# The second quarter of the pole tables: loaded back from DRAM in round 3 or in round 7

## The chip, the core and the metric

The kernel runs on one core of a Trainium2 chip. A core has a matrix engine (TensorE, in the profile PE, with its weight loads as PEld), a vector engine (VectorE, DVE), an engine for activation functions (ScalarE, ACT), a general engine (GpSimd, POOL) and one that mainly issues DMAs (SyncE, SP). Each engine runs its own instructions in order and waits on semaphores for the others. DMAs are issued from an engine's instruction stream and carried out by 16 DMA engines that all queues share; in this kernel SP's loads go through one queue (q1 in the profile) and POOL's through another (q0).

The metric is the time of one execution in microseconds of device time, as the median of several runs; lower is better.

## The reference

The program normalizes its input with a modulated layer norm, runs it through a long convolution whose kernel comes from a state-space model (S4), adds the result, and passes that through a gated MLP with a spatial gate. What matters here is how the convolution kernel `K` comes out of the poles, for D = 576 channels, N = 128 poles a channel and L = 2048 steps:

```python
dt = jnp.exp(log_dt)[:, None]
A = A_re + 1j * A_im
Bc = B_re + 1j * B_im
Cc = C_re + 1j * C_im
logdA = dt * A
dB = dt * Bc
l = (lambda x, dt: x.astype(dt))(jnp.arange(L), A_re.dtype)
P = jnp.exp(logdA[:, :, None] * l[None, None, :])
K = jnp.einsum("dn,dnl,dn->dl", Cc, P, dB).real
...
y = (lambda x, s, axes=(-2,-1): jnp.fft.irfft2(x, s=s, axes=axes))(Yf, (1, L2), axes=(-2, -1))[:, :, 0, :L]
y = (lambda x, *d: x.transpose(*d))(y, 0, 2, 1) + u * Dskip[None, None, :]
```

`Yf` is the product of the spectra of `K` and of the normalized input `u`.

## The kernel before

The kernel has two large stages. The function `ssm` computes the convolution and takes somewhat over 400 us; the class `Mlp` then does the gated MLP in the rest of the time. The change lies in `ssm`.

**The pole tables.** For each pole `poles` works out the real exponent, the phase for one step, the phase for 64 steps, and the weight's logarithm and phase. To keep precision it splits each number into three bf16 parts, and it stores these into two DRAM buffers, `pa_d` for phases and `pb_d` for exponents. `poles` is called twice: for the first quarter of the channels (`p0`), and for the other three quarters together (`p1`), which is a generator that the main loop advances a little in each of its first rounds; its last stores are recorded in round 2. All these stores are DMAs on POOL.

`poles_load(c, Q)` (line 296) reads one quarter back, in the layout that TensorE needs as weights: three tiles of 112 partitions by 9 groups of 128 poles, `lb` (exponents), `lc` and `la` (phases), each with two DMAs of 48 partitions, and one memset of the unused middle rows of `lb`. The queue `Q` is POOL's. The pool of these tiles has two buffers a name, so two quarters can stand in memory.

**The main loop** (line 703) runs over rounds, called `tick`, of which 36 start a new group of 16 channels each, and a quarter has nine groups. A group `g` passes through these steps:

- `e_unit` (L450 to L454): TensorE multiplies `lb` with a selection table into PSUM, ACT takes the exponential into `et`. It is done for three groups at a time, in every third round.
- `t_unit` (L467 to L484): TensorE forms phases out of `lc` and `la` (L467; for the first ten groups with a rounding trick, L471, and a DVE copy, L479; later with L482 on ACT and L483 on DVE), and L484 clears the sign for the cosine.
- `s_unit`, one round later (L489, L490): sine and cosine on ACT, in place in `ft`.
- `p_unit`, two rounds later (L500 to L503): products of `et` and `ft` on DVE.
- `kg_unit`, `d_unit`, `k1_unit` (L513 to L537): small products on TensorE, copies on ACT and an addition on DVE that give the group's convolution kernel and its first transform, `k1`.

Exponentials and sines are in different tables of ACT, so that ACT loads a table (ACT_TABLE_LOAD) when it changes between them.

In the first eight rounds the loop also normalizes the input. `ln_load` fetches `ln_x` and `mod_load` fetches rows of modulation weights, `wm`, both on SP; `ln_pair` (L433, L435) transforms two blocks and stores them into `u1_d` with two DMAs on POOL (L436, `u_d<-st1o` in the profile); `mod_unit` in rounds 3 to 5 works out a modulation row and stores it with one DMA on POOL (L372, `mod_d<-gar`). From round 9 on the loop loads constants `cst` and the transformed input `u` on SP, and from round 10 on come the steps of the convolution itself: `u_unit` (L580, L581; two DMAs on POOL, L582 and L583, exchange the halves of `uu`), `z_unit` (L592, L593), `v_unit` (L600 to L603). `st4` (round 16, `st<-in_c_st` in the profile) and the first MLP weights, `wst`, are loaded on SP in the same stretch of time.

**What sets the order.** A scheduler places the recorded instructions on each engine, except those issued through `mlp.tied`, which keep the order of the program among each other. The DMAs of `poles` and `poles_load` are tied, the stores of `ln_pair` and `mod_unit` aren't. A DMA on POOL also waits until the DMA eight places before it has landed, since eight completion counters are used in turn.

The second quarter is first needed by group 9, that is by `e_unit(9)` to `e_unit(11)` and `t_unit(9)` of round 9. Before the change it is loaded at the end of round 7.

Of the kernel before, what the change touches and what calls it, by code (L numbers as in the profile page):

```python
# [164 lines left out]
def ssm(tc, I, x1_d, consts_s, dram, mod_d, mlp):  # L165
# [5 lines left out]
    with ExitStack() as ctx:  # L171
# [124 lines left out]
        def poles_load(c, Q):  # L296
            for n, d_, k in (("lb", pb_d, 0), ("lc", pa_d, 0), ("la", pa_d, 3)):
                t_ = tb.tile([112, 9, 128], BF, name=n)
                if n == "lb":
                    Q.memset(t_[32:64], 0.0)  # L300
                for h in range(2):
                    Q.dma_start(t_[64 * h:64 * h + 48], d_[c, h, k:k + 6].rearrange("q (c g n) -> (q c) g n", c=8, g=9))
                lt[n, c] = t_
# [22 lines left out]
        def mod_load(k):  # L326

            if k < 2:
                t = kp.tile([128, 32, 128], F32, name="k1").rearrange("p a b -> p (a b)")
                wmt[k] = [t[:96, 6 * HC * hh:6 * HC * hh + 6 * HC].rearrange("p (k n) -> p k n", k=6) for hh in range(2)]  # L330
            else:
                wmt[k] = [ep.tile([96, 6, HC], F32, name="wm") for hh in range(2)]
            for hh in range(2):
                S.dma_start(wmt[k][hh], I["w_mod"][:, k, hh])
# [7 lines left out]
        def mod_unit(k):  # L342
            wm = wmt.pop(k)
            mpart = ep.tile([128, D], F32, name="mpart", bufs=1)
            pm = ps2()
            for hh in range(2):
                for kt in range(6):
                    j = kt % 4
                    T.matmul(pm[32 * j:32 * j + 32, hh, :HC], ec[:, kt:kt + 1].to_broadcast([96, 32]),
                             wm[hh][:, kt], start=kt < 4, stop=kt >= 2, skip_group_check=True)  # L350
            A.activation(v3(mpart), pm[:, :, :HC], AF.Copy)
            pm = ps2()
            for hh in range(2):
                T.matmul(pm[:, hh, :HC], ones, mpart[:, HC * hh:HC * hh + HC], start=True, stop=True)
            src = pm[:, :, :HC]
            if k == 2:
                A.activation(v3(gar), src, AF.Copy)
            elif k == 1:
                V.scalar_tensor_tensor(v3(cga), src, 1.0, v3(gar), op0=ALU.add, op1=ALU.mult)
            elif k == 0:  # L360
                V.tensor_tensor(v3(sga), src, v3(gar), op=ALU.mult)
                for i in range(2):
                    A.activation(gsp, sga, AF.Copy)
                    V.scalar_tensor_tensor(sga, gsp, msk[:, i:i + 1], sga, op0=ALU.mult, op1=ALU.add)
                A.activation(gsp, sga, AF.Copy)
            else:
                mrow = ep.tile([128, D], F32, name="gar", bufs=1)
                if k == 4:
                    A.activation(v3(mrow), src, AF.Identity, bias=one)
                else:  # L370
                    A.activation(v3(mrow), src, AF.Copy)
                G.dma_start(mod_d[k - 3:k - 2], mrow[0:1])  # L372
# [5 lines left out]
        def ln_load(i):  # L378
            x4s[i] = ep.tile([128, 4, D], F32, name="ln_x")
            S.dma_start(x4s[i], I["x"][:, 4 * i:4 * i + 4])  # L380
# [42 lines left out]
        def ln_pair(b):  # L423
            pair = [ln_rows(b), ln_rows(b + 1)]
            for h in range(2):
                c = slice(HC * h, HC * h + HC)
                o = ep.tile([128, 4, HC], F32, name="st1o")
                pms = [ps2(), ps2()]
                for t, (n, rt, cs) in enumerate(pair):
                    for x, y, st in ((cs, gsp, True), (rt, n, False)):  # L430
                        for g in range(4):
                            rows = slice(32 * g, 32 * g + 32)
                            T.matmul(pms[g // 2][64 * t:64 * t + 64, g % 2, :HC], x[rows], y[rows, c], start=st, stop=not st, skip_group_check=True)  # L433
                for k, pm in enumerate(pms):
                    A.activation(o[:, 2 * k:2 * k + 2], pm[:, :, :HC], AF.Copy)  # L435
                G.dma_start(u1_d[:, b:b + 2, :, :, c].rearrange("g b r k d -> (b r k) g d"), o)  # L436
# [7 lines left out]
        def e_unit(g):  # L444
            c, gi = divmod(g, 9)
            lb = lt["lb", c]
            e = et[g] = tb.tile([128, 1536], F32, name="et", bufs=5)
            pa = ps2()
            for h, (l, r) in enumerate(zip(halves(lb, gi), rows(256, 512))):
                T.matmul(pa[:, h], l, r, start=True, stop=True)  # L450
            A.activation(e[:, :1024].rearrange("p (h n) -> p h n", h=2), pa, AF.Exp)
            pb = ps1()
            T.matmul(pb, lb[:, gi], sel[:, 1024:1536], start=True, stop=True)
            A.activation(e[:, 1024:], pb, AF.Exp)  # L454
# [113 lines left out]
        def cst_load(kg):  # L568
            cst[kg] = cs.tile([128, 8, 128], F32, name="cst%d" % kg)
            S.dma_start(cst[kg], I["c_st"][:, 8 * kg:8 * kg + 8])  # L570
# [132 lines left out]
        for tick in range(NG + 4):  # L703
            if tick == 9:
                early.close()
                cs = ctx.enter_context(tc.tile_pool(name="cs", reuse_waits="tile", bufs=1, side="right"))
                sb = ctx.enter_context(tc.tile_pool(name="sb", reuse_waits="tile", bufs=2, side="right"))
                wpre = ctx.enter_context(tc.tile_pool(name="wpre", reuse_waits="tile", bufs=2, side="right"))
            if 9 <= tick < 13:
                cst_load(tick - 9)  # L710
            if tick == 16:
                st4 = cs.tile([128, 16, 2, 64], F32, name="st4")
                S.dma_start(st4, I["c_st4"])
            if tick in (20, 24):
                mlp.start_load(tick // 4 - 5, wpre)
            todo = plan.get(tick, [])

            def go(fn):
                for f, a in todo:
                    if f is fn:  # L720
                        f(*a)

            def lag(fn, n):
                if 0 <= tick - n < NG:
                    fn(tick - n)

            if tick == 0:
                for g in range(3):
                    e_unit(g)
            go(y_load)  # L730
            go(u_load)
            es = iter(range(tick, tick + 3) if tick % 3 == 0 and 0 < tick < NG else ())

            def e_one():
                for g in es:
                    e_unit(g)
                    break

            if tick < 10:
                go(z_unit)  # L740
                lag(p_unit, 2)
                lag(t_unit, 0)
                lag(s_unit, 1)
                go(v_unit)
                lag(kg_unit, 3)
                go(u_unit)
                lag(k1_unit, 4)
                go(y_unit)
                lag(d_unit, 3)
                if tick == 0:  # L750
                    T = nc.tensor
                for _ in range(3):
                    e_one()
            else:
                go(z_unit)
                lag(p_unit, 2)
                lag(t_unit, 0)
                lag(s_unit, 1)
                lag(kg_unit, 3)
                lag(k1_unit, 4)  # L760
                go(y_unit)
                go(v_unit)
                e_one()
                go(u_unit)
                lag(d_unit, 3)
                e_one()
                e_one()
            if tick < 5:
                next(p1, None)
                next(p1, None)  # L770
            if tick == 0:
                mod_load(3)
            if 3 <= tick < 6:
                mod_unit(tick)
                if tick < 5:
                    mod_load(tick + 1)
            j = tick
            if j < 8:
                if j in (2, 4):
                    ln_stats(j // 2 + 1)  # L780
                ln_pair(2 * j)
                if j < 6:
                    r1_load(j + 2)
                if j in (1, 3):
                    ln_load(j // 2 + 2)
            if tick in (7, 13, 21):
                poles_load(1 + (tick > 7) + (tick > 13), mlp.tied.gpsimd)


        tabs.close()  # L790
# [1429 lines left out]
```

## Time and profile before

| | |
|---|---|
| time, median of 3 runs | 1779.78 us (1778.59 to 1780.67) |
| the profiled execution: its time | 1784.37 us |
| the profiled execution: its span | 1782.6 us |
| mean granted clock of TensorE | 0.967 |
| busy: PE | 1669.4 us (94%) |
| busy: DVE | 1259.5 us (71%) |
| busy: ACT | 832.1 us (47%) |
| busy: POOL | 244.5 us (14%) |

All times inside the profile are microseconds from the start of the span. A line of the timeline gives the start, the busy time, the engine, the line of the kernel, the operation, what it writes and reads, its shapes and how many alike were merged; in brackets stands how long the engine was idle just before, and what it was that ended this. A line of the list of waits says who waited for whom, the sum in microseconds, how many times, and the longest. A line of the list of DMA issues gives the queue, the count, the size of one, and the median time from issue to landing.

### The profile page before, as it was taken

The page shows a single profiled execution, that of the slowest core. Times are in us where ns is not written, and L with a number is a line of the kernel's source. Part 1 is how long each engine was busy: PE and PEld are TensorE (multiplying, and loading weights), DVE is VectorE, ACT ScalarE, POOL GpSimd, SP SyncE. Part 2 cuts the span into 40 slices and gives each one's busy share as a digit, 9 for nine tenths or more (in the row PEclk, how much of TensorE's full clock was granted, in tenths as well). Part 3 has the DMA queues.
Part 4 walks back from the last instruction along what each step waited for, and adds up shares of the span by engine and source line. Part 5 has one row for each costly group of instructions (what it writes and reads, how often), then busy time and mean ns, then how long its engine had stood idle before and what let it go on. Part 6 is the DMA issues. An engine that isn't in the chain of part 4 may idle for free.

```text
span 1782.6 us, 36406 instructions
## 1 busy us (share of the span) xinstructions
PE 1669.4 (94%) x15174; PEld 1247.6 (70%) x15174; DVE 1259.5 (71%) x2259; ACT 832.1 (47%) x1118; POOL 244.5 (14%) x400
## 2 busy tenths in 40 slices
PE   3687899997899999999989999999999999999999
PEld 1243556665455445777878888888888888888887
DVE  6874899966898998688899677688344478344432
ACT  4766998844567656445434444234222223122210
POOL 3322232333122211000000000000111100111100
PEclk9587999998999999999999999999999999999999
DMA  9466646679688779767665886873767573556531
GB/s 259 134 178 184 188 121 181 184 216 294 205 255 259 248 230 266 285 245 251 233 222 165 278 302 244 269 247 124 250 219 231 195 235 98 192 195 217 193 111 40
DMA packets 183381, 376.24 MB, mean 211 GB/s; under 512 B 39360, under 2 KB 103488, under 8 KB 182448
## 3 DMA queue, kind: packets, MB, share of 16 engines
q1 hardware_dynamic: 140416, 175.23, 32.5%
q0 software_dynamic: 36896, 172.01, 29.3%
q10 hardware_dynamic: 5904, 26.67, 3.7%
q8 instruction: 119, 1.95, 0.5%
q14 instruction: 46, 0.38, 0.1%
HBM read 263.11 MB, written 101.31 MB: 204 GB/s over the span
## 4 chain that ended last, share of the span: by engine, by line
PE 65%; DVE 14%; DMA 7%; ACT 5%; issue 5%; POOL 2%; SPq 1%; ACTq 0%; DVEq 0%; POOLq 0%
PE ps L152 53%; PE pz L152 2%; DVE zset L152 2%; PE pk L513 2%; DVE bsz L152 2%; PE pk L530 2%; DMA wsst<-in_w_spT 1%; PE pk L592 1%; DVE gt L152 1%; DMA ln_x<-in_x 1%; DMA zset<-set_d 1%; PE pk L600 1%; DVE wsp L152 1%; DVE n L152 1%; DVE rq L152 1%
## 5 line engine op out<-in xcount | busy, mean ns | idle before, releaser
L152 PEld LDWEIGHTS <-zset 128*128 128x128 f16 x7182 | 702.7, 98 | 92.8 <-DVE zset L152 8.1
L152 PE MATMUL ps<-wsp,zset 128*128 128x256 f16 x6048 | 668.9, 273 | 7.1 <-DVE zset L152 6.5
L152 PE MATMUL pz<-wz,nt 128*128 128x512 f16 (+1 forms) x1120 | 224.1, 360 | 12.9 <-ACT nt L152 5.9
L152 PEld LDWEIGHTS <-nt 128*128 128x128 f16 x1120 | 109.5, 99 | 121.3 <-ACT nt L152 7.5
L152 ACT ACTIVATE z<-gt 128x1024 f16<-128x1024 f32 x56 | 59.0, 1054 | 289.6 <-DVE gt L152 289.6
L152 DVE SCALAR_TENSOR_TENSOR gt<-ps,sc,bsp 128x512 f32<-128x512 f32 x36 | 27.0, 749 | 205.0 <-PE ps L152 203.3
L1928 POOL DMA_DIRECT2D zset<-set_d x96 | 50.8, 530 | 869.7 <-PE ps L152 616.3
L152 PE MATMUL ps<-wout,z 128*128 128x288 f16 x1344 | 170.0, 286 | 0.0
L152 PEld LDWEIGHTS <-z 128*128 128x128 f16 x1344 | 131.5, 98 | 33.0
L152 DVE TENSOR_TENSOR raw<-raw 128x512 f32<-128x512 f32 (+2 forms) x228 | 119.1, 528 | 13.6 <-DMA raw<-z_d 9.3
L152 PE MATMUL ps<-n2o,zset 128*128 128x256 f16 x1134 | 128.2, 273 | 0.0
L152 DVE SCALAR_TENSOR_TENSOR gt<-ps,sc,gt 128x512 f32<-128x512 f32 (+1 forms) x180 | 122.2, 696 | 7.6
L152 DVE TENSOR_TENSOR zset<-raw,zset 128x1792 f16<-128x1792 f32 x48 | 96.9, 2019 | 14.3 <-ACT zset L152 14.3
L152 ACT ACTIVATE zset<-raw 128x1792 f16<-128x1792 f32 x48 | 81.1, 1690 | 54.7 <-PE ps L152 22.2
L152 DVE TENSOR_TENSOR z<-ps,z 128x512 f32<-128x512 f32 (+1 forms) x126 | 71.9, 598 | 36.8 <-ACT z L152 25.0
L152 ACT ACTIVATE wsp<-raw,sc 128x1792 f16<-128x1792 f32 x25 | 44.6, 1784 | 42.7 <-DVE raw L152 35.0
L152 ACT ACTIVATE z<-z,sc 128x1024 f32<-128x1024 f32 x21 | 24.1, 1148 | 75.6 <-DVE z L152 71.9
L152 ACT ACTIVATE z<-pz,sc 128x512 f32<-128x512 f32 (+1 forms) x96 | 51.7, 581 | 13.1 <-PE pz L152 7.1
L152 ACT ACTIVATE z<-z,nm,r 128x1152 f32<-128x1152 f32 x24 | 31.5, 1342 | 52.0 <-DVE nm L152 30.7
L152 PE MATMUL ps<-n2q,wf 128*128 128x512 f16 x252 | 55.7, 379 | 0.0
L501 DVE TENSOR_TENSOR pg<-et,ft 128x1024 f32<-128x1024 f32 x36 | 43.8, 1217 | 12.8 <-ACT ft L489 12.7
L152 DVE BATCH_NORM_STATS2 bsz<-z 128x6 f32<-128x384 f32 x96 | 48.4, 546 | 6.2 <-ACT z L152 5.8
(357 smaller groups left out, 2473.0 us busy)
## 6 DMA issues: line engine op xcount, KB each, us to landing
zset<-set_d POOLq DMA_DIRECT2D x96, 896.0 KB, 4.9
raw<-z_d SPq DMA_DIRECT2D x48, 512.0 KB, 5.6
set_d<-zset ACTq DMA_DIRECT2D x24, 896.0 KB, 5.9
z_d<-z POOLq DMA_DIRECT2D x32, 576.0 KB, 9.6
zset<-wa_d POOLq DMA_DIRECT2D x18, 896.0 KB, 4.9
raw<-in_w_spT SPq DMA_DIRECT2D x25, 512.0 KB, 4.3
set_d<-zset SPq DMA_DIRECT2D x12, 896.0 KB, 5.3
u_d<-st1o POOLq DMA_DIRECT2D x16, 576.0 KB, 4.2
```

The lines of the kernel that those rows point to most:

```text
L152: return self.tc.keep_in_program_order(f(*a, **k))
L501: V.tensor_tensor(pr, pi, c3[:, :, None, :].to_broadcast([128, 16, 2, 32]), op=ALU.mult)
L513: T.matmul(pm[32 * j:32 * j + 32, 64 * i:64 * i + 64], x_[:, c], y_[:, c].rearrange("p s j -> p (s j)"), start=st, stop=not st, skip_group ...
L530: T.matmul(pm[64 * ri:64 * ri + 64, 128 * i:128 * i + 128], kk[:, i], r1[ri], start=True, stop=True, skip_group_check=True)
L592: T.matmul(pm[:, w * j:w * j + w], cst[k // 8][:, k % 8], k1t[c][:, k, :w], start=True, stop=True)
L600: T.matmul(pm, inva, zz[:, 0], start=True, stop=False)
L1928: self.nc.gpsimd.dma_start(o, self.set_d[f, j - 1] if j else self.wa_d[f])
```

## The change

```diff
@@ -783,8 +783,8 @@
                     r1_load(j + 2)
                 if j in (1, 3):
                     ln_load(j // 2 + 2)
-            if tick in (7, 13, 21):
-                poles_load(1 + (tick > 7) + (tick > 13), mlp.tied.gpsimd)
+            if tick in (3, 13, 21):
+                poles_load(1 + tick // 10, mlp.tied.gpsimd)
```

`poles_load(1)` is called at the end of round 3 instead of round 7. The calls of rounds 13 and 21 load quarters 2 and 3 as before (13 // 10 = 1 and 21 // 10 = 2). The function is the same, so one memset and six DMAs of 108 KB each are moved; none is added or removed.

The order of instructions in the built program changes as follows.

- POOL: the memset and the six DMAs stand after the two stores of `ln_pair` in round 3 and ahead of ten DMAs that came before them until now: two of `mod_d` and eight of `u_d`.
- PE: the phases of group 9 (L471, L467 with `lc` and `la`) come right after those of group 8, and the exponents of groups 9 and 10 (L450, L453) follow directly; before, these products were mixed with the small products L513 and L530 of earlier groups, and the phases of group 9 came in pieces.
- DVE: L479 of group 9 comes before the products L500 to L503 of group 8 instead of after them.
- ACT: L489 and L490 of group 8 come before the copy L537; the exponentials of groups 9 to 11 are not interrupted; L516, L537 and L581 come after the sines of group 9 and no longer ahead of L482 of group 10.
- SP: the first 1 MB load of `wst` is ahead of one load of `u` and no longer behind it, and another load of `u` moves between two loads of `wst`.

## The prediction

> **What bounds the kernel now.** I read the page first, then busy time and granted clock by stretch, then the waits around 155 to 215 us, and last the single instructions there.
>
> ```profile
> span 1782.6 us, 36406 instructions
> ```
>
> ```profile
> 160.00:165.00 5.00, 0.58 (x1) 0.10 (x1) 3.12 (x4) 1.75 (x2) 0.96 (x2) 0.50 1.03 285
> 165.00:170.00 5.00, 4.49 (x67) 2.33 (x70) 0.00 (x0) 2.00 (x3) 0.00 (x0) 0.50 1.07 294
> 170.00:180.00 10.00, 9.21 (x138) 5.08 (x130) 4.50 (x6) 8.00 (x10) 1.04 (x2) 0.86 0.53 155
> ...
> 220.00:260.00 40.00, 37.22 (x514) 22.01 (x512) 37.93 (x48) 37.09 (x51) 8.56 (x16) 1.00 0.37 108
> ```
>
> The columns are the stretch, its length, then busy us of PE, PEld, DVE, ACT and POOL, the granted TensorE clock, the DMA share and GB/s. From 220 to 260 three engines are busy for 37 to 38 of 40 us, DVE most: nothing there can be made up, so time lost or won earlier is carried on. From 160 to 170 all stand nearly idle and only the DMA engines are full. The waits (us in total, times, longest) and the instructions name the cause:
>
> ```profile
> PE ps L450 <- DMA lb<-pb_d: 7.6, 2, 7.0
> ```
>
> ```profile
> DVE ft L479 <- PE ps L467: 10.1, 1, 10.1
> ```
>
> ```profile
> ACT et L451 <- PE ps L450: 7.9, 3, 4.4
> ```
>
> ```profile
> 164.34 0.58 PE L450 MATMUL ps<-sel,lb 48*128 48x512 bf16 x1 [7.04 <-DMA lb<-pb_d]
> ```
>
> ```profile
> 173.20 1.23 DVE L479 COPY ft<-ps 128x1024 f32<-128x1024 f32 x1 [10.08 <-PE ps L467]
> ```
>
> ```profile
> 156.30 1.08 POOL L152 MEMSET lb<- 32x1152 bf16 x1
> 157.67 1.31 POOL L152 DMA_DIRECT2D lb<-pb_d  x2 [0.29 <-POOL lb L152]
> ```
>
> ```profile
> 159.96 1.00 POOL L152 DMA_DIRECT2D la<-pa_d  x2
> ```
>
> The second quarter is fetched from 157.7 us and wanted at once. PE waits 7.0 + 0.6 us for it, ACT 7.9 us for PE, and DVE stands 10.1 us before it can copy the tenth group's phases (L479).
>
> **The change part by part.** Moved are one memset and six DMAs, two each for `lb`, `lc` and `la`. The built order puts them on POOL behind the store pair of round 3, ahead of ten stores which they followed before. Here are that place and what lies around it (PE's `wm` products are those of the last modulation row, `mod_unit(5)`), then DMA landings (count, KB each, us from issue to landing):
>
> ```profile
> 89.39 3.74 POOL L152 DMA_DIRECT2D pa_d<-pt  x6 [1.25 <-DVE mv L409]
> ```
>
> ```profile
> 103.00 0.52 POOL L372 DMA_DIRECT2D mod_d<-gar  x1 [9.11 <-ACT gar L371]
> ```
>
> ```profile
> 107.44 0.76 POOL L436 DMA_DIRECT2D u_d<-st1o  x1 [1.44 <-ACT st1o L435]
> ```
>
> ```profile
> 113.91 0.53 POOL L372 DMA_DIRECT2D mod_d<-gar  x1 [5.71 <-ACT gar L369]
> ```
>
> ```profile
> 115.09 1.18 DVE L408 BATCH_NORM_STATS2 bs<-ln_x 128x6 f32<-128x288 f32 x3 [5.30 <-DMA ln_x<-in_x]
> ```
>
> ```profile
> 108.93 1.30 SPq L334 DMA_DIRECT2D wm<-in_w_mod  x2
> ```
>
> ```profile
> 124.48 2.62 PE L349 MATMUL ps<-wm,ec 96*32 96x288 f32 x18
> ```
>
> ```profile
> u_d<-st1o POOLq DMA_DIRECT2D x1, 576.0 KB, 9.7
> ```
>
> ```profile
> wm<-in_w_mod SPq DMA_DIRECT2D x1, 648.0 KB, 11.1
> ```
>
> ```profile
> 110.00:120.00 10.00, 6.63 (x106) 3.49 (x95) 4.91 (x14) 8.80 (x13) 1.72 (x3) 1.00 1.00 330
> ```
>
> Issue: by the rows at 156.30 to 159.96 the block takes 1.08 + 0.29 + 1.31 + 1.00 + 1.00 = 4.7 us of POOL. It starts at 108.2 (107.44 + 0.76) and ends near 112.9, before the `mod_d` store that came at 113.91 after 5.7 idle us. Cost 0; without that cover 4.7 us on a store that nothing reads until the next stage. Can the block itself hang? It reads what `poles` stored, whose last DMA issue ended at 93.1 (89.39 + 3.74), and each DMA takes the completion counter of the one eight places ahead of it; the youngest of these is the `mod_d` store of 103.0. Both are old by 109. A knock-on: the first `u_d` store behind the block takes the counter of the store that lands at 117.1 (107.44 + 9.7), about 1 us after it would go out. Its tile is rewritten only in round 5, near 133 us: cost 0.
>
> DMA traffic: 6 x 108 = 648 KB now come into the stretch 110 to 120, which is full already (share 1.00). The neighbour to fear for is `ln_x`: it lands at 115.1 and DVE stands 5.3 us for it. At that stretch's 330 GB/s 648 KB are 2.0 us, the upper bound; the lower bound is 0. Which end? In the old place the POOL loads came in by order of issue:
>
> ```profile
> lb<-pb_d POOLq DMA_DIRECT2D x2, 108.0 KB, 6.8
> ```
>
> ```profile
> la<-pa_d POOLq DMA_DIRECT2D x2, 108.0 KB, 8.9
> ```
>
> `lb`, out from 157.7, is in at about 165; `la`, out from 160.0, at about 169. So in the new place they stand behind the `u_d` store on POOL's queue, which lands at 117.1, after `ln_x`. I take 0 and keep 2.0. `wm`'s second half goes out at 109.6 (108.93 and half of 1.30), lands at 120.7 and is used at 124.5, so 2.0 us there are hidden.
>
> The Trainium skill, DMA: Bandwidth & Descriptors, section Queues, rings and completion order, says that each DMA engine takes turns between the queues that have work, a packet at a time, and starts what is in one ring in order. By it the POOL queue already holds its turn with the `u_d` store, so `ln_x` loses nothing until 117 (0 in the sum); had that queue been empty, the turns would cost up to the 2.0. The row of `la` behind `lb` agrees with the second half of this.
>
> What is won: in the built order PE makes the tenth group's phases (L471, L467) and the exponents (L450, L453) right behind the ninth group's phases, and ACT does L489, L490, L537, a table load, three pairs L451 and L454, then L482. ACT becomes what sets the pace, since PE's pieces in it are under 2 us each. Its rows, with those of the next steps:
>
> ```profile
> 158.38 1.15 ACT L489 ACTIVATE ft<-ft,consts_s 128x1024 f32<-128x1024 f32 x1 [0.43 <-DVE ft L484]
> ...
> 160.49 1.28 ACT L451 ACT_TABLE_LOAD   x1
> 166.15 1.02 ACT L451 ACTIVATE et<-ps 128x1024 f32<-128x1024 f32 x1 [4.38 <-PE ps L450]
> 167.07 1.08 ACT L454 ACTIVATE et<-pk 128x512 f32<-128x512 f32 x2
> ...
> 175.27 0.60 ACT L581 ACTIVATE uu<-pk 128x512 f32<-128x512 f32 x1 [0.34 <-PE pk L580]
> 175.76 1.11 ACT L482 ACTIVATE ft<-ps,consts_s 128x1024 f32<-128x1024 f32 x1
> ...
> 180.19 1.09 ACT L482 ACTIVATE ft<-ps,consts_s 128x1024 f32<-128x1024 f32 x1
> ```
>
> ```profile
> 184.07 2.07 PE L592 MATMUL pk<-k,cst 128*128 128x128 f32 x8 [4.86 <-ACT k L537]
> ```
>
> ```profile
> 186.93 1.22 DVE L593 TENSOR_TENSOR zz<-pk,uu 128x1024 f32<-128x1024 f32 x1
> ```
>
> ```profile
> 176.16 0.53 POOL L582 DMA_DIRECT2D uu<-uu  x1 [15.20 <-ACT uu L581]
> ```
>
> ```profile
> uu<-uu POOLq DMA_DIRECT2D x2, 128.0 KB, 7.2
> ```
>
> From 158.38: L489 and L490 take 2.11 (160.49 - 158.38), L537 0.49 (as L581 to L482, 175.76 - 175.27), the table load 1.3, three pairs at 0.92 (167.07 - 166.15) plus 0.49, together 4.2. L482 starts at 166.5 instead of 175.76: 9.3 us earlier. The next L482 came 4.43 later (180.19 - 175.76); the new order puts L516, L537 and L581 ahead of it, at most 3 x 0.49, say 1.3. So 166.5 + 4.43 + 1.3 = 172.2 against 180.19: 8.0 earlier. PE's first `z_unit` (L592) came 3.88 after that and comes at 176.1: also 8.0 earlier.
>
> But what is late next? DVE's L593 needs L592, done at 178.1 (176.1 + 2.07), and the swapped halves of `uu`. L581 now goes at 171.7 (172.2 - 0.49); the two swap DMAs follow it by 0.9 and 1.4 (176.16 and half a microsecond more, against 175.27), so the second is out at 173.1. Landing took 7.2 us while `st4` and the `wst` loads were in flight, and these move along with the swap: it lands at 180.3. L593 then runs at 180.3 instead of 186.93: 6.6 us earlier. An unloaded queue would bring the halves before 178.1, and the wait of 2.2 us would be gone.
>
> Sum: DVE is the busiest engine of the stretch that follows, so its 6.6 are carried; 0 for POOL, 0 for `ln_x`. The profiled execution took 1784.37 us, 1.8 more than its span; less 6.6 it would be 1777.8. The runs' median is 4.6 lower than that execution, and I assume the same shift there: **1779.78 - 6.6 = 1773.2 us.** Lower gain: PE's own wait 7.6, less 2.0 for `ln_x`, less 2.2 for the swap, 3.4: 1776.4. Upper gain: all of DVE's 10.1: 1769.7.
>
> On SP one 1 MB `wst` load now precedes a `u` load that is used several rounds later: 0; 1 MB takes 3 us at 330 GB/s, and if the rounds between did not cover them, they would be the price. At 157 to 170 the `u` and `cst` loads lose a competitor of 648 KB; the first `u` was not what ACT waited for (0.34 at L581): 0.
>
> **The rivals.** *Absorbed.* Another operand takes the stall's place, in the conv stage or where that stage hands over to the gated MLP, or the loads still come late. For it: DMA is full from 155 to 170 with `u` and `cst` as well. Against: PE waited for `lb` alone there, and POOL's new place has no late wait. Time 1779.8, unchanged.
>
> *Slower: TensorE's clock.* The clock row shows 0.50 from 160 to 170 and 0.86 from 170 to 180. Should the new pattern of short PE bursts keep it at half speed into the full stretch behind 200 us, PE's 37.22 busy us of 40 (at 1.00) would become 74, a loss of 34 us per 40. The gain is eaten after 6.6 / 34 x 40 = 8 us of half clock there, and it is slower by over 3.6 from 12 us on; 15 us would give 1779.8 + 6 = 1786. For it: the clock does fall after each idle piece. Against: with far more idle time before it, it was at 1.00 from 220 on, and the change takes idle time away.
>
> On that, the Trainium skill (TensorE: Matmul & The Clock Gate, Part 1: The HAM clock gate) says that an idle window of some 3.4 us halves the clock and a like time of steady work restores it. The 0.50 behind the 7.04 us gap agrees; by this rule the half clock cannot last 12 us in a full stretch.
>
> **How the numbers follow.** A measurement of this kernel tells about 0.2%, 3.6 us, from no change. Forecast (gain 3.4 to 10.1): 0.80. A gain beyond 10.1, if the removed idle time also spares cold TensorE work: 0.03. Absorbed: 0.12. Slower: 0.05. So faster 0.83, same 0.12, slower 0.05. The likeliest case's own range, 1769.7 to 1776.4, already holds 0.80; I give 1769.0 to 1776.5.
>
> **What would show it.** Right: the `lb` load is issued on POOL near 109 us; DVE's wait for `ln_x` stays near 5.3 (7.3 would be the upper bound of the contention); no wait of PE for `lb` and none of 10 us before L479; first L592 near 176 us; DVE waits about 2 us for `uu` before its first L593; everything behind 200 us is the old profile shifted by 6 to 8 us. Wrong: a wait of 3 us or more at another place between 110 and 200, a shift at 220 us that is gone at 450, or a clock below 1.00 from 220 to 260.

## The result and the profile after

The changed kernel took 1770.2 us (median of 7 runs, 1765.67 to 1773.18) beside 1778.8 us for the kernel before on the same chip (7 runs, 1775.77 to 1780.67). The ratio is 0.9947, with a 95% interval of 0.9932 to 0.9962: 0.53% or some 9 us faster. The prediction was 1773.2 us in a range of 1769.0 to 1776.5, a gain of 6.6 us.

The profiled execution took 1773.18 us.

```profile
span 1771.4 us, 36409 instructions
```

The first view is the one by stretches, as before the change: length, busy us of PE, PEld, DVE, ACT and POOL, granted clock, DMA share, GB/s.

```profile
160.00:165.00 5.00, 3.51 (x87) 2.12 (x84) 4.99 (x7) 4.49 (x6) 0.00 (x0) 1.00 1.03 302
165.00:170.00 5.00, 4.21 (x80) 2.39 (x83) 1.05 (x3) 4.98 (x8) 0.00 (x0) 1.00 1.05 339
170.00:180.00 10.00, 5.83 (x60) 3.40 (x48) 9.45 (x12) 9.57 (x13) 1.47 (x3) 0.83 0.79 270
...
220.00:260.00 40.00, 37.78 (x518) 22.26 (x516) 36.89 (x46) 37.09 (x49) 12.26 (x22) 1.00 0.40 114
```

The hole from 160 to 170 is filled: in its first half DVE and ACT are busy for 4.99 and 4.49 of 5 us (3.12 and 1.75 before), in its second ACT for 4.98 (2.00). DMA is as full as it was, and TensorE's clock is at 1.00 there instead of 0.50. Next, the waits from 105 to 205 us (who for whom, sum, times, longest):

```profile
DVE bs L408 <- DMA ln_x<-in_x: 4.9, 1, 4.9
...
DVE ft L479 <- PE ps L467: 3.6, 3, 1.6
...
POOL u_d L436 <- DMA u_d<-st1o: 2.7, 1, 2.7
PE ps L450 <- ACT et L451: 2.6, 2, 1.3
```

No wait of PE for `lb` is left, and DVE's longest wait for the phases is 1.6 us where it was 10.1. POOL's new place, on the timeline:

```profile
104.77 0.52 POOL L372 DMA_DIRECT2D mod_d<-gar  x1 [9.62 <-ACT gar L371]
...
109.96 1.08 POOL L152 MEMSET lb<- 32x1152 bf16 x1
111.33 1.06 POOL L152 DMA_DIRECT2D lb<-pb_d  x2 [0.29 <-POOL lb L152]
112.39 0.99 POOL L152 DMA_DIRECT2D lc<-pa_d  x2
113.37 0.99 POOL L152 DMA_DIRECT2D la<-pa_d  x2
115.72 0.49 POOL L372 DMA_DIRECT2D mod_d<-gar  x1 [1.35 <-ACT gar L369]
118.88 0.79 POOL L436 DMA_DIRECT2D u_d<-st1o  x1 [2.67 <-DMA u_d<-st1o]
```

Its first row matters for all that follows: this store came at 103.00 before and comes at 104.77 here, ahead of the moved block. So this execution was 1.77 us late before the change could act, and each start in it is to be reduced by 1.77 before it is compared. The chain that follows the loads, on ACT, PE and DVE:

```profile
160.73 1.15 ACT L489 ACTIVATE ft<-ft,consts_s 128x1024 f32<-128x1024 f32 x1 [0.48 <-DVE ft L484]
...
168.78 1.17 ACT L482 ACTIVATE ft<-ps,consts_s 128x1024 f32<-128x1024 f32 x1
...
174.48 1.12 ACT L482 ACTIVATE ft<-ps,consts_s 128x1024 f32<-128x1024 f32 x1
```

```profile
178.98 1.16 PE L592 MATMUL pk<-k,cst 128*128 128x128 f32 x8
```

```profile
180.17 1.23 DVE L593 TENSOR_TENSOR zz<-pk,uu 128x1024 f32<-128x1024 f32 x1
187.18 1.22 DVE L593 TENSOR_TENSOR zz<-pk,uu 128x1024 f32<-128x1024 f32 x1 [0.51 <-PE pk L592]
195.16 1.22 DVE L593 TENSOR_TENSOR zz<-pk,uu 128x1024 f32<-128x1024 f32 x1
```

Before the change the third L593 and, at the start of the MLP stage, POOL's memset of `wz` stood here:

```profile
202.61 1.22 DVE L593 TENSOR_TENSOR zz<-pk,uu 128x1024 f32<-128x1024 f32 x1
```

```profile
407.48 2.02 POOL L152 MEMSET wz<- 64x2304 f16 x1
```

and after it here:

```profile
400.03 2.02 POOL L152 MEMSET wz<- 64x2304 f16 x1
```

Counted from the `mod_d` store, the third L593 came 99.61 us later before the change (202.61 - 103.00) and 90.39 after it (195.16 - 104.77): 9.22 us earlier. From there to the memset it is 204.87 us in both (407.48 - 202.61 and 400.03 - 195.16), equal to a hundredth of a microsecond. So what is won by the third L593 is carried whole through the rest of the stage, and nothing is added. The span shrank by 11.2 us: 9.2 here, less the 1.8 lost ahead of the block, and 3.7 behind the memset, which the next section finds to be scatter.

### The profile page after: what moved, and what is told of

It is laid out like the page before. It is cut to its first block, busy times and chain, and to the rows that moved or that the text cites. A ratio compares the mean times of both kernels' runs of the same rounds, so it can differ in the third digit from the quotient of the medians.

```text
span 1771.4 us, 36409 instructions
## 1 busy us (share of the span) xinstructions
PE 1666.3 (94%) x15174; PEld 1244.5 (70%) x15174; DVE 1259.8 (71%) x2259; ACT 831.7 (47%) x1118; POOL 244.1 (14%) x400
## 4 chain that ended last, share of the span: by engine, by line
PE 62%; DVE 16%; issue 7%; DMA 6%; ACT 5%; POOL 2%; SPq 1%; ACTq 0%; POOLq 0%; DVEq 0%
PE ps L152 54%; DVE bsz L152 2%; DVE n L152 1%; PE pk L530 1%; DVE zset L152 1%; PE pk L513 1%; DVE gt L152 1%; DVE rq L152 1%; DMA ln_x<-in_x 1%; DMA zset<-set_d 1%; PE pk L592 1%; DVE wso L152 1%; DMA wst<-in_w_in 1%; DMA k<-in_w_mod 1%; PE pk L600 1%
## 5 line engine op out<-in xcount | busy, mean ns | idle before, releaser
L152 PE MATMUL ps<-wout,z1b 128*128 128x288 f16 x384 | 52.6, 286 | 0.5 <-ACT z1b L152 0.5
L501 DVE TENSOR_TENSOR pg<-et,ft 128x1024 f32<-128x1024 f32 x36 | 43.8, 1217 | 11.5 <-ACT ft L489 11.4
```

Source lines behind the costliest of these rows:

```text
L152: return self.tc.keep_in_program_order(f(*a, **k))
L501: V.tensor_tensor(pr, pi, c3[:, :, None, :].to_broadcast([128, 16, 2, 32]), op=ALU.mult)
```

## The experiments

Whole times of one kernel scatter by 5 us and more from run to run. A better ruler for one profile is the distance from the `mod_d` store near 103 us to the third L593 and to the `wz` memset. It is read in each profile as just shown; the ratios are to the kernel before on the same chip.

| kernel | ratio (95% interval) | to the third L593, us | to the memset, us |
|---|---|---|---|
| before (first profile, second profile) | 1 | 99.61, 101.10 | 304.48, 305.97 |
| after (three profiles) | 0.9947 (0.9932 to 0.9962) | 90.39, 89.52, 89.56 | 295.26, 294.40, 294.43 |
| round6 | 0.9948 (0.9934 to 0.9963) | 90.01 | 294.88 |
| round7 | 0.9934 (0.9918 to 0.9951) | 89.39 | 294.26 |
| ahead_of_stores | 0.9944 (0.9925 to 0.9963) | 89.37 | 294.26 |
| lb_alone | 0.9966 (0.9952 to 0.9981) | 95.13 | 299.75 |
| phases_alone | 0.9964 (0.9951 to 0.9978) | 96.75 | 301.63 |
| later_by_5 | 1.0044 (1.0030 to 1.0058) | 106.62 | 311.60 |
| swap_late | 0.9937 (0.9917 to 0.9957) | 94.20 | 299.07 |

The theory was that the lateness of the second quarter alone cost time. Its rivals: that the new compute order brings the gain, that the place in the fourth round matters for itself (its neighbours there pay part back), or that the wait which the profile names, PE for `lb`, is the whole cause.

**Both kernels once more (before2, after2, after3).**

> The kernel before, unchanged, as a control: ratio 1.000, interval within 0.998 to 1.002. Its profile is a second look at the lengths of the stages. If the 1.5 us between the wz memset and the first n_d store, and the 2.2 us in the gated MLP, that the changed kernel was shorter in its profile are variation from execution to execution, this profile differs from the first one of the same kernel by a like amount in those stages; if they belong to the change, the two profiles of the kernel before agree there within 0.5 us.

> The changed kernel, unchanged, beside the others on one chip: ratio 0.993 to 0.996. By the theory the conv stage (first u_d store at 94 us to the wz memset near 400 us) is again 8 to 9 us shorter than in the profiles of the kernel before, and the gated MLP's stages differ from profile to profile by as much as two profiles of the kernel before differ from each other.

> The changed kernel, unchanged, on the same chip as the late swap: ratio 0.9935 to 0.995; first swap of uu in 4.5 to 5.5 us, no wait of L593 over 0.5 us.

before2 has the ratio 1.0002 (0.9990 to 1.0014). after2 has 0.9942 (0.9925 to 0.9960) and, in another series, after3 0.9929 (0.9909 to 0.9949). In the ruler the two profiles of before lie 1.5 us apart and the three of after 0.9; the change lies between them with 9.2 (the least distance) to 11.6. From the memset to the end of the span it is 1375.1 us (1782.6 - 407.48) and 1370.8 in before and before2, 1371.4, 1371.4 and 1368.5 in the three of after. So the same kernel differs by 4.3 us there: the 3.7 us of the first pair of profiles aren't the change's.

**The load in the sixth or seventh round, tick 5 or 6 (round6, round7).** The compute engines keep the order of the changed kernel.

```diff
-            if tick in (3, 13, 21):
+            if tick in (5, 13, 21):
```

```diff
-            if tick in (3, 13, 21):
+            if tick in (6, 13, 21):
```

> The second quarter is loaded in the sixth round (tick 5), two rounds later than in the changed kernel and two rounds earlier than before; the compute engines and SP get the same order of instructions as in the changed kernel. The block then stands on POOL near 139 us, ahead of four u_d stores, and lands by about 155 us; PE wants la and lc near 158 and lb near 161. Theory (only the lateness of the second quarter cost time): the whole gain, 1770 us, a ratio to the kernel before of 0.995, within 1.5 us of the changed kernel; DVE's wait for ln_x near 115 us stays at 4.9 us. Rival 1 (in the fourth round the 648 KB hurt their neighbours, and the gain shown is what is left): up to 2 us faster than the changed kernel, and a shorter wait for ln_x. Rival 2 (the place in the fourth round matters for another reason than the arrival, such as the stores' counters): at least 2 us slower than the changed kernel.

> The same with the load in the seventh round (tick 6), one round earlier than before. The compute order is that of the changed kernel. The block stands on POOL near 150.5 us and lands behind a u_d store: lb near 161, lc near 162.5, la near 165 us. Theory: la is some 7 us late for PE, which holds L450 back behind it from 160.8 to about 165, and ACT's first L451 from 164.6 to about 166.5: 1 to 3 us of the gain are lost, ratio 0.996 to 0.9965; a wait of PE on la or lb of 3 to 7 us shows. Rival (any place ahead of the eighth round gives the whole gain, since the compute order brings it): the same time as the changed kernel although PE waits for la. Rival (a late load costs its lateness one for one): 5 us or more of the gain lost, ratio 0.998.

Both give the whole gain, by ratio and by ruler. For round7 the theory's size was wrong: no wait for `la` came, and nothing was lost. The block was issued from 145.86 to 150.40 us, and the DMA view of that stretch (queue, count, KB of one, median us to landing) says why:

```profile
lb<-pb_d POOLq DMA_DIRECT2D x2, 108.0 KB, 3.6
lc<-pa_d POOLq DMA_DIRECT2D x2, 108.0 KB, 3.4
la<-pa_d POOLq DMA_DIRECT2D x2, 108.0 KB, 3.1
```

The expectation had reckoned with 9 to 12 us, as the loads took in the crowd of the fourth round. In a gap of the DMA traffic they land in 3.1 to 3.6, ahead of PE's need near 154 (the tenth group's first L467 with `la` is at 154.41). One round earlier than before would have been enough. That rules out a gain that belongs to the fourth round. These runs don't rule out the compute order, which is the same in both as in the changed kernel.

**One half of the tables alone (lb_alone, phases_alone).** `poles_load` gets an argument with the names to load.

```diff
-            if tick in (3, 13, 21):
-                poles_load(1 + tick // 10, mlp.tied.gpsimd)
+            if tick in (3, 7, 13, 21):
+                poles_load(1 + tick // 10, mlp.tied.gpsimd, {3: "lb", 7: "lc la"}.get(tick, "lb lc la"))
```

phases_alone has `{3: "lc la", 7: "lb"}` instead.

> Only lb (the exponents' table) and its memset go in the fourth round; lc and la (the phases' tables) stay in the eighth, issued near 156.5 and 157.5 us. Theory (the stall ends when the last of the three tables is in, and then ACT's chain from there): PE no longer waits for lb, but the tenth group's phases wait for la until about 165 us, DVE copies them (L479) near 167 to 170 instead of 173.2, and 3 to 7 of the some 9 us are won: ratio 0.996 to 0.998. Rival (the wait that the profile names, PE for lb, is the whole cause): the whole gain, ratio 0.9945, although la is late.

> Only lc and la go in the fourth round; lb and its memset stay in the eighth, with lb landing near 164 us as before. Theory: ACT's first L451 comes near 166 as before, but L482 follows 4.2 us behind it as in the changed kernel and not 9.6, because the phases are ready: L482 some 5.4 us earlier than before, 3 to 4 us later than in the changed kernel; ratio 0.9965 to 0.998. Rival (lb is the whole cause): no gain, ratio 0.999 to 1.001, with the wait of PE for lb still near 7 us.

Each gave a part, as the theory had it (the ratio of phases_alone, 0.9964, lies just below the range expected): by the ruler to the memset, lb_alone won 4.7 to 6.2 us against the two profiles of before, phases_alone 2.9 to 4.3. In lb_alone the wait moved to the phases' tables, as the timelines of PE and of DVE show:

```profile
161.75 0.39 PE L467 MATMUL ps<-sel,lc 48*128 48x256 bf16 x1 [3.63 <-DMA lc<-pa_d]
```

```profile
166.12 1.23 DVE L479 COPY ft<-ps 128x1024 f32<-128x1024 f32 x1 [2.95 <-PE ps L467]
```

In phases_alone PE waits for `lb` nearly as long as before, and still 3 to 4 us are won (timelines of PE and of ACT):

```profile
164.81 1.32 PE L450 MATMUL ps<-sel,lb 48*128 48x512 bf16 x3 [6.92 <-DMA lb<-pb_d]
```

```profile
172.91 1.11 ACT L482 ACTIVATE ft<-ps,consts_s 128x1024 f32<-128x1024 f32 x1 [0.77 <-PE ps L467]
```

L482 stands 6.74 behind the first L451 (at 166.17), where the expectation had 4.2 and the kernel before 9.6 (175.76 - 166.15). So the wait that the profile names isn't the whole cause: the phases' tables were late as well, and PE's wait for them shows only where the first wait is gone, in lb_alone (3.63 us).

**Still later (later_by_5).** The kernel before, with more memsets ahead of the second quarter's DMAs:

```diff
-                    Q.memset(t_[32:64], 0.0)
+                    [Q.memset(t_[32:64], 0.0) for _ in range(6 if c == 1 else 1)]
```

> The kernel before, with the memset of lb done six times in the second quarter's load instead of once: 5 x 1.08 = 5.4 us more on POOL ahead of the three tables, nothing else added; the compute order behind the load is replanned. Theory (lateness is paid for): 3 to 6.5 us slower than before, ratio 1.0017 to 1.0036, PE's wait for lb longer by up to 5.4 us. Rival (the arrival is hidden by other late work, and the gain of the change comes from the new compute order): within 1 us of before unless the new order itself costs.

It is slower by 0.44%, 8 us, which is more than the 6.5 expected at most; its interval begins at 5.3. The timelines of POOL and PE have the smaller figure:

```profile
153.70 7.05 POOL L152 MEMSET lb<- 32x1152 bf16 x6
```

```profile
167.89 0.58 PE L450 MATMUL ps<-sel,lb 48*128 48x512 bf16 x1 [11.35 <-DMA lb<-pb_d]
```

The memsets took 7.05 instead of 1.08, so the DMAs went 6.0 us later, and the memset of `wz` comes 5.6 to 7.1 later: one for one, within the scatter. So over all these kernels the time follows the arrival of the tables.

The scheduler plans a new compute order for each of the last three, so order and arrival aren't wholly separated. phases_alone comes near to it. From 95 to 215 us its trace has PE's lines in the order of the changed kernel, and ACT and DVE differ from that order in a few places only (on ACT the tenth group's L489 comes ahead of the exponentials, at 160.26). With this order and a late `lb`, 6.4 to 7.2 us are missing against the three profiles of after (301.63 beside 295.26, 294.40 and 294.43). So the new order alone doesn't bring the gain. Whether it has a share in the 2.9 to 4.3 us that phases_alone does win is not shown: there DVE copies the tenth group's phases at 157.66 (L479), ahead of the wait for `lb`, which it can do only with their tables in.

The replanned kernels have other waits as well: lb_alone has two more ACT table loads of 1.28 us (at 159.47 and 162.88), which fall into the time in which the phases' tables are waited for. At the first L593 DVE waits 1.79 us for PE's L453 in lb_alone, 2.34 for a DMA in phases_alone and 2.61 for the exchange of `uu` in later_by_5; the kernel before has no wait there. So the shares that these three kernels show hold to 2 or 3 us and no closer.

**Ahead of the round's stores (ahead_of_stores).**

```diff
-            j = tick
+            j = tick; tick == 3 and poles_load(1, mlp.tied.gpsimd)
...
-            if tick in (3, 13, 21):
+            if tick in (13, 21):
```

> The load stays in the fourth round, but ahead of that round's two u_d stores on POOL instead of behind them; the other engines keep the order of the changed kernel. The 648 KB then are on POOL's queue near 104 us, just when ln_x is loaded, and the u_d stores go out some 4.7 us later. Theory (POOL's queue is served in order, and what stands in it does not change what ln_x gets): DVE's wait for ln_x 4 to 5.5 us, time within 1.5 us of the changed kernel, ratio 0.993 to 0.996. Rival (the load's bytes hold ln_x up, 2.0 us at most): wait for ln_x 6 to 7 us, and up to 2 us of the gain lost. The late u_d stores cost nothing by either.

The whole gain again. DVE's wait for `ln_x` was 4.48 us:

```profile
112.69 1.18 DVE L408 BATCH_NORM_STATS2 bs<-ln_x 128x6 f32<-128x288 f32 x3 [4.48 <-DMA ln_x<-in_x]
```

With the load in the fourth round that wait was 4.85, 5.03, 4.20, 4.48 and 5.03 us (after, after2, after3, ahead_of_stores, swap_late); with it elsewhere 5.30, 3.96, 4.14, 4.08 and 4.84 (before, before2, round6, round7, later_by_5). The means are 4.7 and 4.5, so no price of the 648 KB can be told from this scatter, and the 2.0 us of the upper bound are excluded.

**A late swap (swap_late).** The prediction let the first L593 wait 2.2 us for the exchanged halves of `uu`; in the changed kernel it waits 0.00, 0.36 and 0.25. Here that wait is made: `st4`'s load goes to POOL's queue between the two halves.

```diff
+        st4_load = lambda: mlp.tied.gpsimd.dma_start(st.setdefault("st4", cs.tile([128, 16, 2, 64], F32, name="st4")), I["c_st4"])
...
-            G.dma_start(uu[:64, 1], uu[64:, 0])
-            G.dma_start(uu[64:, 1], uu[:64, 0])
+            g = mlp.tied.gpsimd if (c, i) == (0, 0) else G; g.dma_start(uu[:64, 1], uu[64:, 0])
+            (c, i) == (0, 0) and st4_load(); g.dma_start(uu[64:, 1], uu[:64, 0])
...
-                st4 = cs.tile([128, 16, 2, 64], F32, name="st4")
-                S.dma_start(st4, I["c_st4"])
+                st4 = st.pop("st4")
```

> The changed kernel with the 1 MB load of st4 taken from SP's queue and put on POOL's between the two halves of the first uu swap, so that the second half stands behind it; nothing else moves, and st4 is read tens of microseconds later. It lets the first L593 wait for the swap, as the prediction assumed it would (2.2 us). Theory (the first L593 starts a stretch in which DVE is full, so its delay is carried to the end): the second half lands 3 to 5 us later than in the changed kernel, L593 starts 2 to 5 us later, and the whole takes as much longer: ratio to the kernel before 0.9955 to 0.997 where the changed kernel has 0.9942. Rival (the delay is made up behind L593): L593 late by 2 us or more, but the stage's end within 1 us and the ratio within 0.0006 of the changed kernel's.

DVE's timeline:

```profile
184.51 1.23 DVE L593 TENSOR_TENSOR zz<-pk,uu 128x1024 f32<-128x1024 f32 x1 [4.51 <-DMA uu<-uu]
```

Against after3, L593 starts 6.5 us later from the `mod_d` store (184.51 - 103.20 = 81.31; 177.67 - 102.86 = 74.81). By the third L593 4.6 of these are left (94.20 and 89.56), and at the memset still 4.6 (299.07 and 294.43). So some 2 us of such a delay are made up within two steps, and the rest is carried to the end of the stage: the rival is out by this profile. The times don't resolve it: 0.9937 (0.9917 to 0.9957) beside 0.9929 for after3, where 4.6 us would be 0.0026. Both ratios lie below the ranges expected for them, and that of the late swap is nearer to what the rival expected, so the finding rests on one profile.

No version beats the changed kernel by more than the measurements can tell; round7 (0.9934) and it agree within their intervals and have the same ruler.

## Why the prediction was right, and which size was off

**The cause was the late table, and the stall went.** Shown by the four places that all win (tick 3 ahead of and behind the stores, ticks 5 and 6), by the halves, which win a part each, by the later load, which loses one for one, and by phases_alone, which has nearly the new order of the compute engines and lacks 6.4 to 7.2 us of the gain while `lb` is late.

**POOL's issue costs nothing.** Right. The block ended at 114.36 (113.37 + 0.99) and the `mod_d` store followed at 115.72, 10.95 us behind the one before it (10.91 before the change). The first `u_d` store behind the block went out 3.16 us after that `mod_d` store (118.88 - 115.72) where it was 2.20 before the change (116.11 - 113.91), so it was 0.96 us late; the prediction had about 1. Its 2.67 idle us above also hold the time in which its data wasn't ready, which was 1.67 before. In after2 and after3 it was 1.2 and 1.9 us late. ahead_of_stores, which pushes a later store back by some 3.5 us (to 121.35, from 117.78 in round7), loses nothing either.

**Contention with `ln_x` taken as 0.** Right within the scatter of the wait. Whichever bytes stood first in POOL's queue, the stores' or the load's, the wait was the same. That fits the turns between queues of which the prediction spoke (the Trainium skill, DMA: Bandwidth & Descriptors, Queues, rings and completion order), but a scatter of 1.3 us proves nothing of it.

**ACT's chain.** First L482 forecast 9.3 us earlier, measured 8.8 (175.76 - 168.78 + 1.77 = 8.75); second 8.0, measured 7.5 (180.19 - 174.48 + 1.77); first L592 8.0, measured 6.9 (184.07 - 178.98 + 1.77). In this pair of profiles each is right to about a microsecond. That is partly luck: in before2 the first L482 comes 2.7 us later than in before (75.46 and 72.76 us behind the `mod_d` store), and in the three profiles of after it comes 64.01, 63.18 and 63.19 us behind it. L592 lost 1.1 because PE stood ahead of it behind DVE, which now has products of an earlier group first:

```profile
174.94 1.82 PE L530 MATMUL pk<-small,kab 128*64 128x128 f32 x16 [3.29 <-DVE kab L520]
```

Right behind this gap of 3.29 us the granted clock was at 0.50 once more, from 175.2 to 178.4; these L530 took 1.82 us where such a block took 1.09 before (at 176.74), and the two L580 behind them 2.04 where it was 1.12 (at 177.76). L592 itself ran at 1.00 again and took 1.16 instead of 2.07; the prediction counted the old duration, at half clock. So the clock is at 1.00 from 160 to 175 where the large hole was, and a short hole of the new order halves it for some 3 us. That fits, nearly, the rule that the prediction quoted from the Trainium skill (TensorE: Matmul & The Clock Gate, Part 1: The HAM clock gate): this gap is slightly under its 3.4 us.

**The swap: the term that was mis-sized.** The prediction said that `st4` and `wst` "move along with the swap", so that its landing would take 7.2 us as before and DVE would wait 2.2 us at L593. The swap landed in 4.7 us (5.1 and 5.0 in after2 and after3), and DVE's L593 started without a wait. SP's rows, of before and then of after, show what did not move along:

```profile
161.06 14.56 SPq L574 DMA_DIRECT2D u<-u_d  x3
175.85 0.34 SPq L713 DMA_DIRECT2D st<-in_c_st  x1
```

```profile
163.03 6.37 SPq L574 DMA_DIRECT2D u<-u_d  x3
...
169.63 0.34 SPq L713 DMA_DIRECT2D st<-in_c_st  x1
170.03 0.43 SPq L908 DMA_DIRECT2D wst<-in_w_in  x1
```

```profile
uu<-uu POOLq DMA_DIRECT2D x2, 128.0 KB, 4.7
```

SP was held at the `u` loads by the same stall and came free 8.0 us sooner (175.85 - 169.63 + 1.77), the swap only 3.0 (176.16 - 174.89 + 1.77). So the 1 MB loads, once 0.3 us ahead of the swap, now go 5 us ahead of it. That the `u` loads were held by buffers that PE's L580 frees is argued from the code, not tried. Without the 2.2 the prediction's own chain ends with L592 at 178.1, 75.1 us behind the store at 103.00; measured are 75.40. But that the two are so near is partly luck, since L593 also stood in DVE's own queue. DVE had work without a break from an L501 that waits for ACT's sine up to the first L593, 7.56 us of it before the change (186.93 - 179.37) and 7.73 after it (180.17 - 172.44):

```profile
179.37 1.23 DVE L501 TENSOR_TENSOR pg<-et,ft 128x1024 f32<-128x1024 f32 x1 [0.51 <-ACT ft L489]
```

```profile
172.44 1.23 DVE L501 TENSOR_TENSOR pg<-et,ft 128x1024 f32<-128x1024 f32 x1 [0.52 <-ACT ft L489]
```

This L501 came 8.70 us earlier (179.37 - 172.44 + 1.77), as the first L482 did (8.75). So the gain went from ACT's chain to L593 through DVE's own queue, a path that the prediction didn't follow. L592 was done 0.8 us before DVE came to L593 in the kernel before (184.07 + 2.07 beside 186.93), and just as DVE came to it in the changed one (178.98 + 1.16 beside 180.17). In after2 and after3 the wait for `uu` adds 0.36 and 0.25 us to it.

The remaining gain from 8.53 at the first L593 (186.93 - 180.17 + 1.77) to 9.22 at the third lies between these two: 15.68 us before, 14.99 after. That is within the scatter of one kernel: it is 14.48 in before2.

**Carried on.** That the gain is carried is right, and shown by the 204.87 us from the third L593 to the memset, which before2, after2, after3, round6, round7, ahead_of_stores and swap_late have too, within 0.02. That it is DVE which carries it is not shown: from 220 to 260 us after the change PE is the busier of the two (37.78 of 40 us, DVE 36.89).

**The rivals.** Nothing absorbed the gain, and the clock was at 1.00 from 220 to 260, so the slower case didn't occur. One of the prediction's signs of being wrong did appear, waits of 3 us or more that the kernel before doesn't have: DVE stands 3.95 us at 169.98 for ACT's L482, and PE the 3.29 us at 174.94. The first is ACT's chain, which the prediction itself had as what sets the pace; the second was over before DVE came to L593. By the ratio the gain was 9.4 us (0.0053 x 1778.8), near the upper end of the range from 3.4 to 10.1: that bound, all of DVE's wait before L479, was nearer than the sum.

## What to carry to other kernels

A stall that all engines share can also hold the engine that issues loads, as it seems to have held SP here, so what is in flight beside a later transfer changes when the stall goes; a landing time read next to a stall isn't to be taken over into a forecast without it. Of several tables that arrive together the profile names only the wait for the first, and repairing that one alone gave about half of the gain. Where whole times scatter as much as the effect, the distance between two instructions on either side of it, in one profile, told about 1.5 us here where single times scattered by 5 and more.

## What was not expected of the hardware

The same 128 KB exchange of `uu` on POOL's queue took 7.2 us to land with a 1 MB load issued on SP 0.3 us ahead of it (before), 4.7 with two of them issued 5 us ahead (after), and 2.2 in round7, where one had gone out 5.3 us ahead (165.14 and 170.44) and the other went only afterwards:

```profile
uu<-uu POOLq DMA_DIRECT2D x2, 128.0 KB, 2.2
```

With the two 1 MB loads issued about 3 us ahead it took 6.5 and 6.6 us (lb_alone and phases_alone). As an estimate from these rows, an even sharing between the two queues would make it about twice the 2.2, 4.4 us; the 7.2 behind a load just issued is more than that. What makes the difference was not tried.
